# Linear attention feeding a routed expert layer: rests of the kv sums on row halves, one PSUM ring for two projections, and a new hand-made list of steps

## The chip, the core and the metric

The kernel runs on one core of one Trainium2 chip. The metric is the time of one execution in microseconds (us), the median of several runs. The engines named below are TensorE (PE in the profile, its weight loads PEld), VectorE (DVE), ScalarE (ACT), GpSimd (POOL) and the queue that issues most transfers (SP).

## What is computed

Attention without a softmax over positions, for 8 batches x 8 heads of 576 positions, and then a layer of 8 experts in which each of the 4608 tokens goes to one expert:

```python
def phi(x):
    proj = np.einsum('bhsd,df->bhsf', x, w_phi)
    proj = proj - np.max(np.abs(proj), axis=-1, keepdims=True)
    return np.concatenate([np.exp(proj), np.exp(-proj)], axis=-1)
q_p, k_p = phi(q), phi(k)
kv  = np.einsum('bhsf,bhsd->bhfd', k_p, v)
z   = np.sum(k_p, axis=2)
num = np.einsum('bhsf,bhfd->bhsd', q_p, kv)
den = np.einsum('bhsf,bhf->bhs', q_p, z)[..., None] + 1e-06
x = (num / den)                        # then tokens x 512
logits = x @ w_gate + modality_bias[modality_id]
e_idx = argmax(logits); gate = softmax(logits)[e_idx]
out[mask] = gate * (relu(x[mask] @ w1[e]) @ w2[e])     # for each expert e
```

## The kernel before

The 64 heads are worked in 16 groups of four heads (two pairs); a group's number is the `qi` behind the dot in the list of steps below. For each group there are these steps, and each step is one part of a Python generator, so that steps of different groups can be recorded between one another:

- `K0`, `K1`, `K2`: the projection of k. `K0` and `K1` take four tiles of 128 positions, `K2` the last 64 positions of each pair. Parts: matmuls into PSUM (`pk`, L557), the largest absolute value (`mk`, DVE L561), its subtraction (`dk`, DVE L566), two exponentials into `kp` (ACT L572).
- `Q0`, `Q1`: the projection of q for a pair. Matmuls into `pq` (L584) and a copy to SBUF (`d`, ACT L588), twice; the largest over partitions (`mq`, GpSimd L592); a subtraction (DVE L595); two exponentials into `qp` (ACT L601).
- `V`: the sums kv and z. For each sign `s` of the exponential and each head `a`: two matmuls of the rest, the last 64 positions of both pairs (L613; `vb` holds the rests of v of both pairs side by side with zeros, so 130 columns move through weights of 128 rows x 64 columns), then 16 matmuls over the eight full tiles (L617, 65 columns each). One PSUM tile for each `s`, each copied by ACT (L623).
- `T`: kv is transposed (`kvT`, L633), copied, and multiplied with the gate's weights (L642), and DVE puts the result back beside kv.
- `N0` to `N3` and `L`: numerator, denominator and gate sums for 128 positions (`pn`, L668) or for the rests (`pl`, L687). DVE divides and SP stores x (`xs` L676, `xl` L697).
- `XR`, `XL`, `R`: logits and the places of the tokens in the experts' lists, eight times with four or five tiles of tokens (`Route.group`).

The rest of the list (`SU`, `F`, `E`, `W`, `M`, `S`, `Y`, `U`, ...) is the routing plan and the first two slots of the expert layer. After it the expert layer runs slot by slot in a fixed order (`Experts.slots`), which the change leaves alone.

The order is a list written out as text (`ORDER`), 1153 words such as `K2.0`; `program` goes through it and records one part of the named step, and each engine then does its instructions in that order, waiting only for what it needs. Loads of k, q and v aren't in this list: `step` records the load of a group two places on as soon as the last matmul that reads the buffer has been recorded (`READS`). PSUM has eight banks: a ring of four one-bank tiles, `pm`, for `V`, `T`, `N`, `L` and small things; one two-bank tile `pk`; one two-bank tile `pq`.

Ahead of the list stand the loads of groups 0 and 1, and the constructors of `Numbers`, `Route` and `Attention`: 12 and then 16 matmuls on a tile of ones (L88, L102), small DVE operations that make indices, and fills of `pad` and `xg` by GpSimd.

An fp32 matmul shows in the trace as two records. A shape such as `128*64` is the weights' rows and columns; weights of 64 rows (`64*128`) use a half of the array's rows, those of 64 columns a half of its columns, and two halves can be at work at a time.

## Time and profile before

| | us |
|---|---|
| median of 3 runs (lowest 712.62, highest 714.45) | 714.27 |
| the profiled execution | 713.8 |
| its span, from the first to the last instruction | 712.0 |
| PE busy in the span | 696.6 |
| DVE busy | 562.9 |
| ACT busy | 453.0 |
| GpSimd busy | 278.9 |

The first 260 us are the attention steps, then the expert layer takes over. The records of matmuls are pipelined: one lasts some 220 ns while the next begins 30 ns later, so a busy PE in this table can still be waiting, and it is read from starts of blocks and from the waits. A row of the timeline is: start, length of the whole merged piece, engine, line, operation, output and input, number of records, and in brackets the idle time ahead of it.

### The profile page before, as it was taken

To read this page: it belongs to the slowest core of one execution; us is meant where nothing else is said; L and a number is where in the kernel's file an instruction comes from. 1 tells how busy PE (TensorE), PEld (TensorE's weight loads), DVE (VectorE), ACT (ScalarE), POOL (GpSimd) and SP (SyncE) were. 2 spreads that over 40 slices of the span, in tenths; PEclk is the share of its full clock that TensorE was granted. 3 is DMA by queue.
4 is the path that set the end of the run, shared out by engine and by line. 5 is a ranking of instruction groups with operands and counts; after the bars stand their busy time and mean duration, and the time that the engine had idled before them with its cause. 6 is when DMAs were issued, how large, how long until landed. Compare 5 with 4: busy or idle time off the path is not lost.

```text
span 712.0 us, 21360 instructions
## 1 busy us (share of the span) xinstructions
PE 696.6 (98%) x8678; PEld 602.6 (85%) x8678; DVE 562.9 (79%) x1287; ACT 453.0 (64%) x744; POOL 278.9 (39%) x161
## 2 busy tenths in 40 slices
PE   7999999999999999999999999999999999999995
PEld 5889888898888899988888888878888888888884
DVE  7888879899999988579987787768568568678774
ACT  4888688777985883445755576547447447455742
POOL 4555446465445722488742410321131131222122
PEclk9999999999999999999999999999999999999998
DMA  9655555565554668566676739995998984476411
GB/s 217 174 160 159 158 149 152 141 165 159 159 159 111 203 239 276 176 245 205 195 253 237 258 137 417 414 415 181 385 337 330 392 294 139 168 286 227 169 45 32
DMA packets 70321, 155.16 MB, mean 218 GB/s; under 512 B 16698, under 2 KB 45502, under 8 KB 58432
## 3 DMA queue, kind: packets, MB, share of 16 engines
q1 hardware_dynamic: 62208, 134.61, 56.2%
q0 software_dynamic: 7552, 18.92, 7.4%
q8 instruction: 72, 1.18, 0.7%
q14 instruction: 41, 0.34, 0.1%
q10 hardware_dynamic: 448, 0.11, 0.1%
HBM read 135.96 MB, written 19.55 MB: 218 GB/s over the span
## 4 chain that ended last, share of the span: by engine, by line
PE 80%; issue 8%; DVE 6%; ACT 2%; POOL 1%; DMA 1%; SPq 0%; POOLq 0%; ACTq 0%; DVEq 0%
PE p L895 19%; PE p L875 13%; PE pn L668 9%; PE pv L617 7%; PE p L877 6%; PE pq L584 5%; PE pk L557 5%; PE p L858 3%; DVE l L823 3%; PE pv L613 2%; PE pt L831 2%; PE pt L895 2%; PE pt L1005 1%; PE up L991 1%; PE kvT L633 1%
## 5 line engine op out<-in xcount | busy, mean ns | idle before, releaser
L823 DVE TENSOR_TENSOR l<-raw,h 128x1024 fp32r<-128x1024 f32 x148 | 177.1, 1218 | 13.0 <-ACT h L821 12.8
L592 POOL PARTITION_ALL_REDUCE mq<-d x32 | 130.8, 4089 | 115.2 <-ACT d L588 89.9
L821 ACT CAST h<-raw 128x1024 fp32r<-128x1024 f32 x148 | 149.2, 1049 | 3.0 <-PE pt L895 2.2
L875 PE MATMUL p<-xx,h 128*128 128x512 f32 x512 | 140.1, 395 | 0.2 <-issue 0.2
L878 ACT COPY ts<-p 128x256 f32<-128x256 f32 x128 | 47.7, 373 | 110.5 <-PE p L877 109.9
L779 POOL DMA_INDIRECT xg<-x,me x40 | 48.4, 1210 | 163.8 <-PE pt L831 81.4
L895 PE MATMUL p<-h,hh 128*128 128x512 f32 x272 | 107.4, 395 | 0.0
L895 PE MATMUL p<-l,hh 128*128 128x512 f32 x272 | 106.1, 390 | 0.7 <-DVE l L823 0.7
L895 PE MATMUL p<-h,hl 128*128 128x512 f32 x272 | 106.0, 390 | 0.0
L879 DVE TENSOR_TENSOR ts<-ts,p 128x256 f32<-128x256 f32 x128 | 53.5, 418 | 59.5 <-ACT ts L878 59.5
L875 PEld LDWEIGHTS p<-xx,h 128*128 128x128 f32 x512 | 88.0, 189 | 14.3 <-issue 2.0
L877 PEld LDWEIGHTS p<-xx,l 128*128 128x128 f32 x512 | 78.6, 189 | 11.4 <-DVE l L823 0.5
L783 POOL DMA_INDIRECT out_dram<-os,me x36 | 45.7, 1270 | 99.6 <-DVE os L942 72.7
L877 PE MATMUL p<-xx,l 128*128 128x256 f32 x512 | 81.7, 281 | 0.3 <-DVE l L823 0.3
L572 ACT ACTIVATE kp<-dk 128x1024 f32<-128x1024 f32 (+1 forms) x96 | 74.7, 837 | 6.4 <-DVE dk L566 6.3
L668 PE MATMUL pn<-kv,qp 128*64 128x73 f32 x2048 | 73.9, 227 | 0.4 <-DVE kv L645 0.4
L668 PEld LDWEIGHTS pn<-kv,qp 128*64 128x64 f32 x2048 | 68.4, 136 | 5.6 <-issue 2.8
L601 ACT ACTIVATE qp<-d 128x1152 f32<-128x1152 f32 x64 | 71.0, 1159 | 1.4 <-DVE d L595 1.1
L617 PE MATMUL pv<-va,kp 128*64 128x65 f32 x2048 | 70.7, 221 | 0.7 <-issue 0.7
L617 PEld LDWEIGHTS pv<-va,kp 128*64 128x64 f32 x2048 | 68.7, 137 | 0.8 <-issue 0.8
L881 ACT ACTIVATE hh<-ts 128x256 fp32r<-128x256 f32 x128 | 54.1, 423 | 14.3 <-DVE ts L879 14.2
L588 ACT COPY d<-pq 128x576 f32<-128x576 f32 x64 | 40.7, 636 | 32.6 <-PE pq L584 31.6
(234 smaller groups left out, 1109.0 us busy)
## 6 DMA issues: line engine op xcount, KB each, us to landing
raw<-in_w_dram SPq DMA_DIRECT2D x92, 1024.0 KB, 7.0
qt<-in_qT_dram SPq DMA_DIRECT2D x30, 288.0 KB, 4.5
va<-in_vm_dram SPq DMA_DIRECT2D x16, 512.0 KB, 5.1
x<-xs SPq DMA_DIRECT2D x64, 128.0 KB, 3.7
kt<-in_kT_dram SPq DMA_DIRECT2D x15, 512.0 KB, 4.6
kt<-in_kT_dram SPq DMA_DIRECT2D x16, 64.0 KB, 4.7
vb<-in_vt_dram SPq DMA_DIRECT2D x32, 32.0 KB, 4.3
x<-xl SPq DMA_DIRECT2D x32, 32.0 KB, 2.8
```

What stands on the lines that cost most here:

```text
L572: nc.scalar.activation(kp[:, 4 * u:4 * u + T, :, s, :].rearrange("p t a f -> p a t f"), dk, AF.Exp, scale=sc)
L592: self.line.put(nc.gpsimd.partition_all_reduce(mq.rearrange("p a s -> p (a s)"), d.rearrange("p a s -> p (a s)"), P, bass_isa.ReduceOp.abs ...
L601: nc.scalar.activation(qp[:, 2 * pr:2 * pr + 2, i, :], d, AF.Exp, scale=sc)
L617: nc.tensor.matmul(pt[c:c + CW, k // 4, a], kp[:, k, a, s, c:c + CW], va[:, k // 4, k % 4, h], start=False, stop=k == 7, tile_position=(0, c))
L668: nc.tensor.matmul(pp[c:c + CW, g], q["qp"][:, g, s, P * j + c:P * j + c + CW], q["kv"][:, s, g // 2, 73 * (g % 2):73 * (g % 2) + 73], sta ...
L821: nc.scalar.copy(h, r)
L823: nc.vector.tensor_tensor(l, r, h, ALU.subtract)
L875: nc.tensor.matmul(pp, h1[:, cc, f], self.XX[:, cc].rearrange("p a t -> p (a t)"), start=cc == 0, stop=False)
L877: nc.tensor.matmul(pp[:, 0:256], l1[:, cc, f], self.XH[:, cc], start=False, stop=cc == 3)
L879: nc.vector.tensor_tensor(s, s, pp[:, 0:256], ALU.add)
L881: a = nc.scalar.activation(self.HH[:, j], s, AF.Relu)
L895: nc.tensor.matmul(pp, a[:, f, tk], b[:, f], start=i == 0, stop=i == 23)
```

## The change

- **Rests on row halves.** `va` now has nine tiles; the ninth holds the rest of pair 0 in rows 0 to 63 and that of pair 1 in rows 64 to 127. There is one PSUM tile for each pair `r` (not for each sign), both taken at the beginning of `V`. All eight matmuls of the rests come first, as a part of their own, 64 rows each, with weights of 128 columns and 65 columns moving, the two row halves in turn. `V` has five parts instead of four. `vb` and its zeros are gone, and its two loads are one.
- **One ring.** The projections of k take their tile from `pq`, which gets two buffers; `pk` is gone. Only in group 0 do `K1` and `K2` take `pm` tiles, as before.
- **Loads as steps.** `LK`, `LQ`, `LV`, `LA`, `LB` (halves of the first k), `LP` (projection weights, now half on SP and half on ACT's queue), `LG`, `LM` stand in the list. `READS` is gone.
- **Small work as steps.** `NU`, `NA`, `NR` are the parts of the constructors' small operations. `PI.4` is four matmuls on 64 rows of ones into a `pm` tile; it stands in the list 12 times, eight of them ahead of the first `N`. The 16 matmuls of L102 are gone.
- **Routing by nine tiles.** `R` runs four times with nine tiles instead of eight times with four or five; `low` is made by one DVE operation for nine tiles instead of one for each.
- **The list** is another one, with 1200 words.

```diff
+    def idle(self, n, rows=P):
+        pw = self.ps.tile([P, 512], F32, tag="pm", name="idle")
+        for _ in range(n):
+            self.nc.tensor.matmul(pw[:, 0:256], self.one[:rows], self.one[:rows].unsqueeze(1).to_broadcast([rows, 2, P]), start=True, stop=True)
...
-        for _ in range(WARM2):
-            nc.tensor.matmul(pw[:, 0:256], self.one, self.one.unsqueeze(1).to_broadcast([P, 2, P]), start=True, stop=True)
...
-        for t in range(T0, T0 + T):
-            nc.vector.tensor_scalar(self.low[:, t], self.row, self.lof[:, t:t + 1], None, ALU.is_equal)
+        nc.vector.tensor_tensor(self.low[:, T0:T0 + T], self.row.unsqueeze(1).to_broadcast([P, T, P]),
+                                self.lof[:, T0:T0 + T].unsqueeze(2).to_broadcast([P, T, P]), ALU.is_equal)
...
-        self.va = [lv.tile([P, 2, 4, 130], F32, name=f"va{i}") for i in range(2)]
-        self.vb = [lv.tile([P, 2, 130], F32, name=f"vb{i}") for i in range(2)]
+        self.va = [lv.tile([P, 9, 130], F32, name=f"va{i}") for i in range(2)]
...
+    def load_w(self):
+        for a, e in enumerate((self.nc.sync, self.nc.scalar)):
+            e.dma_start(self.wp[64 * a:64 * a + 64], self.w_phi)
...
-    def load_a(self, qi, vm):
-        self.nc.sync.dma_start(self.va[qi % 2][:, :, :, 1:129], vm[qi])
-
-    def load_b(self, qi, vt):
-        for j in range(2):
-            r = slice(64 * j, 64 * j + 64)
-            self.nc.sync.dma_start(self.vb[qi % 2][r, j, 1:129], vt[qi, r])
+    def load_v(self, qi, vm, vt):
+        va = self.va[qi % 2]
+        self.nc.sync.dma_start(va[:, 8, 1:129], vt[qi])
+        self.nc.sync.dma_start(va[:, 0:8, 1:129], vm[qi].rearrange("p r t d -> p (r t) d"))
...
-            pv = [pk.tile([P, 2, 4, P], F32, tag="pk", name=f"pk{n}_{u}")[:, :, 0:T]]
+            pv = [pq.tile([P, 2, 512], F32, tag="pq", name=f"pk{n}_{u}").rearrange("p a (t f) -> p a t f", f=P)[:, :, 0:T]]
...
-        va, vb, kp = self.va[qi % 2], self.vb[qi % 2], q["kp"]
+        va, kp = self.va[qi % 2], q["kp"]
+        pt = [pm.tile([P, 512], F32, tag="pm", name=f"pv{n}_{r}")[:, 0:260].rearrange("p (s a c) -> p s a c", s=2, a=2)
+              for r in range(2)]
         for s in range(2):
-            pt = pm.tile([P, 512], F32, tag="pm", name=f"pv{n}_{s}")[:, 0:260].rearrange("p (r a c) -> p r a c", r=2, a=2)
             for a in range(2):
-                h = slice(65 * a, 65 * a + 65)
-                for c in range(0, P, CW):
-                    nc.tensor.matmul(pt[c:c + CW, :, a], kp[:, 8, a, s, c:c + CW], vb[:, :, h],
-                                     start=True, stop=False, tile_position=(0, c))
-                for k in range(8):
-                    for c in range(0, P, CW):
-                        nc.tensor.matmul(pt[c:c + CW, k // 4, a], kp[:, k, a, s, c:c + CW], va[:, k // 4, k % 4, h],
-                                         start=False, stop=k == 7, tile_position=(0, c))
-            yield
-            if s == 0:
+                for r in range(2):
+                    i = slice(64 * r, 64 * r + 64)
+                    nc.tensor.matmul(pt[r][:, s, a], kp[i, 8, a, s], va[i, 8, 65 * a:65 * a + 65],
+                                     start=s + a == 0, stop=False)
+        yield
+        for r in range(2):
+            for s in range(2):
+                for a in range(2):
+                    for k in range(4):
+                        for c in range(0, P, CW):
+                            nc.tensor.matmul(pt[r][c:c + CW, s, a], kp[:, 4 * r + k, a, s, c:c + CW],
+                                             va[:, 4 * r + k, 65 * a:65 * a + 65],
+                                             start=False, stop=s + a + k == 5, tile_position=(0, c))
+            yield
+            if r == 0:
                 q["kv"] = w.tile([P, 2, 2, 146], F32, tag="kv", name="kv" + n)
-            nc.scalar.copy(q["kv"][:, s, :, 8:138], pt.rearrange("p r a c -> p r (a c)"))
+            nc.scalar.copy(q["kv"][:, :, r, 8:138], pt[r].rearrange("p s a c -> p s (a c)"))
             yield
...
-    K2.0 K2.0 SU.0 SU.0 K0.0 K0.0 Q0.0 Q0.0 K2.0 K1.0 Q0.0 K2.0 Q0.0 Q0.0 K0.0 K0.0 K0.1 K1.0 K0.1 Q1.0 Q1.0 Q1.0 Q1.0
+    NU.0 NU.0 LA.0 LP.0 NU.0 LQ.0 NU.0 NU.0 K0.0 NU.0 LB.0 PI.4 NA.0 NA.0 NA.0 K0.0 Q0.0 K1.0 K0.0 K2.0 Q0.0 Q1.0 NU.0
...
-        pk = pool(pr, "pk", "right", space=PSUM)
-        pq = pool(pr, "pq", "right", space=PSUM)
+        pq = pool(pr, "pq", "right", bufs=2, space=PSUM)
...
+                if u == "PI":
+                    num.idle(qi, 64)
+                    continue
```

What the new list makes of the order is seen at three places. The first is PE at the start of the program. Before, from the last of the L102 matmuls to the first full tiles of `V` of group 0 (the first number behind `pk`, `pq` and `pv` is the group):

```order
L557 MATMUL pk0_2_0_257<-wp_126,kt0_234 128x128
L557 MATMUL pk0_2_1_258<-wp_126,kt0_234 128x128
L557 MATMUL pk0_0_270<-wp_126,kt0_234 128x128 x8
L584 MATMUL pq0_0_0_281<-qt0_238,wp_126 128x288 x2
...
L584 MATMUL pq0_1_1_334<-qt0_238,wp_126 128x288 x2
L584 MATMUL pq1_0_0_341<-qt1_249,wp_126 128x288 x2
L557 MATMUL pk1_1_351<-wp_126,kt1_243 128x128 x8
L613 MATMUL pv0_0_371<-vb0_207,kp0_305 64x2x65 x2
L617 MATMUL pv0_0_371<-va0_205,kp0_305 64x65 x16
```

And now, from the same engine's first projection to the same tiles:

```order
L585 MATMUL pk0_0_174<-wp_76,kt0_164 128x128 x8
...
L612 MATMUL pq0_0_0_197<-qt0_169,wp_76 128x288 x2
...
L612 MATMUL pq0_1_1_249<-qt0_169,wp_76 128x288 x2
L585 MATMUL pk1_0_262<-wp_76,kt1_246 128x128 x8
...
L585 MATMUL pk1_1_292<-wp_76,kt1_246 128x128 x8
L113 MATMUL numbers_301<-mean_273,free_70 128x8
L650 MATMUL pv0_0_280<-va0_128,kp0_255 64x65 x32
L650 MATMUL pv0_1_281<-va0_128,kp0_255 64x65 x32
```

The same projections stand ahead of `V` of group 0; the first is `K0` instead of `K2`, and the 16 matmuls on ones ahead of it are gone, while four-matmul idle pieces (left out here) stand between.

The second is PE in the middle of the attention part, around `V` of group 10. Before:

```order
L613 MATMUL pv10_0_3370<-vb0_207,kp10_3005 64x2x65 x2
L617 MATMUL pv10_0_3370<-va0_205,kp10_3005 64x65 x16
L613 MATMUL pv10_0_3370<-vb0_207,kp10_3005 64x2x65 x2
L617 MATMUL pv10_0_3370<-va0_205,kp10_3005 64x65 x16
L687 MATMUL pl9_3407<-kv9_3008,qp9_3110 64x73 x8
L557 MATMUL pk11_2_3424<-wp_126,kt11_2832 128x128 x2
L584 MATMUL pq11_0_0_3439<-qt11_2986,wp_126 128x288 x2
L613 MATMUL pv10_1_3446<-vb0_207,kp10_3005 64x2x65 x2
```

Now:

```order
L642 MATMUL pv10_1_3153<-va0_128,kp10_3027 128x65
L612 MATMUL pq11_0_0_3162<-qt11_2726,wp_76 128x288 x2
L702 MATMUL pn9_2_3165<-kv9_2939,qp9_2845 64x73 x16
L721 MATMUL pl9_3182<-kv9_2939,qp9_2845 64x73 x8
L650 MATMUL pv10_0_3152<-va0_128,kp10_3027 64x65 x32
L612 MATMUL pq11_0_1_3237<-qt11_2726,wp_76 128x288 x2
L585 MATMUL pk11_0_3251<-wp_76,kt11_2563 128x128 x8
L702 MATMUL pn9_0_3260<-kv9_2939,qp9_2845 64x73 x16
L650 MATMUL pv10_1_3153<-va0_128,kp10_3027 64x65 x32
```

The rests stand as a block of their own between projections, and both PSUM tiles of `V` are held from there to the end of the second block of L650.

The third is the queue SP around the load of v for group 12 (`va0` in both; `xl9` and `xl10` are stores of group 9 and 10). Before:

```order
L534 DMA va0_205<-in_vm_dram 128x8x128
L539 DMA vb0_207<-in_vt_dram 64x128 x2
L697 DMA x_58<-xl9_3434 64x128 x2
L520 DMA qt13_3626<-in_qT_dram 64x2x576 x2
L697 DMA x_58<-xl8_3364 64x128 x2
...
L676 DMA x_58<-xs10_1_3762 128x256
L697 DMA x_58<-xl10_3790 64x128 x2
```

Now:

```order
L710 DMA x_58<-xs10_1_3718 128x256
L710 DMA x_58<-xs10_0_3686 128x256
L731 DMA x_58<-xl10_3730 64x128 x2
L566 DMA va0_128<-in_vt_dram 128x128
L567 DMA va0_128<-in_vm_dram 128x8x128
L559 DMA kt14_3838<-in_kT_dram 128x2x512
```

The load of v for group 12 stood ahead of group 10's stores of x and now stands behind all of them.

## Rows read from the trace of the kernel before

**Rows 1.** The page: span, and the engines' busy time, share and instructions
```profile
span 712.0 us, 21360 instructions
PE 696.6 (98%) x8678; PEld 602.6 (85%) x8678; DVE 562.9 (79%) x1287; ACT 453.0 (64%) x744; POOL 278.9 (39%) x161
```

**Rows 2.** Busy time by stretches: engine, (instructions), then PE's clock, transfers' share, GB/s
```profile
20.00:40.00 20.00, 19.95 (x459) 17.24 (x456) 16.80 (x37) 17.22 (x25) 8.78 (x4) 1.00 0.54 137
...
220.00:240.00 20.00, 19.81 (x451) 17.04 (x449) 19.70 (x63) 14.86 (x21) 14.68 (x6) 1.00 0.45 127
```

**Rows 3.** Waits of PE, 28 to 300 us: total us, times, longest
```profile
PE pv L617 <- issue: 0.7, 1, 0.7
PE pk L557 <- PE pq L584: 0.5, 2, 0.3
PE pn L668 <- DVE kv L645: 0.4, 1, 0.4
```

**Rows 4.** Waits of PE from 300 us to the end
```profile
PE p L895 <- DVE l L823: 0.7, 1, 0.7
PE p L877 <- DVE l L823: 0.3, 1, 0.3
PE p L875 <- issue: 0.2, 1, 0.2
```

**Rows 5.** Timeline of the start, all engines
```profile
0.75 0.88 SPq L529 DMA_DIRECT2D kt<-in_kT_dram  x2
...
1.34 0.61 ACTq L484 DMA_DIRECT2D wp<-in_w_phi_dram  x1
...
4.62 3.58 PE L102 MATMUL warm<-one 128*128 128x256 bf16 x16
...
8.12 1.54 PE L557 MATMUL pk<-wp,kt 64*128 64x128 f32 x20
...
10.22 0.64 ACT L588 COPY d<-pq 128x576 f32<-128x576 f32 x1 [6.74 <-PE pq L584]
```

**Rows 6.** Transfers of the whole run: times, KB each, median us from issue to landing
```profile
va<-in_vm_dram SPq DMA_DIRECT2D x16, 512.0 KB, 5.1
...
kt<-in_kT_dram SPq DMA_DIRECT2D x2, 256.0 KB, 3.0
...
wp<-in_w_phi_dram ACTq DMA_DIRECT2D x2, 32.0 KB, 3.2
```

**Rows 7.** Chain of work that ended last: start, us, piece
```profile
262.72 11.71 PE p L858 x96
```

**Rows 8.** Timeline of PE, the first `pn`
```profile
27.89 3.25 PE L668 MATMUL pn<-kv,qp 128*64 128x73 f32 x96
```

**Rows 9.** Timeline of PE, 100 to 109 us
```profile
101.15 1.16 PE L557 MATMUL pk<-wp,kt 64*128 64x128 f32 x16
102.14 0.66 PE L584 MATMUL pq<-qt,wp 64*128 64x288 f32 x4
...
103.28 0.59 PE L642 MATMUL kvT<-wgb,kvTs 128*64 128x16 f32 x16
103.72 1.22 PE L668 MATMUL pn<-kv,qp 128*64 128x73 f32 x32
...
105.45 1.06 PE L557 MATMUL pk<-wp,kt 64*128 64x128 f32 x16
106.36 0.76 PE L584 MATMUL pq<-qt,wp 64*128 64x288 f32 x4
...
107.32 1.10 PE L617 MATMUL pv<-va,kp 128*64 128x65 f32 x32
108.25 0.40 PE L613 MATMUL pv<-vb,kp 128*64 128x130 f32 x4
108.48 1.10 PE L617 MATMUL pv<-va,kp 128*64 128x65 f32 x32
```

**Rows 10.** Weight loads by form, 0 to 300 us: count, busy us, mean ns, idle before
```profile
L617 PEld LDWEIGHTS pv<-va,kp 128*64 128x64 f32 x2048 | 68.7, 137 | 0.8 <-issue 0.8
...
L557 PEld LDWEIGHTS pk<-wp,kt 64*128 64x128 f32 x576 | 38.3, 188 | 8.5 <-issue 2.5 <-PE pq L584 1.4 <-DVE dk L566 1.3
```

**Rows 11.** DVE by form, 0 to 300 us, the longest operation
```profile
L595 DVE TENSOR_TENSOR d<-d,mq 128x1152 f32<-128x1152 f32 x32 | 46.0, 1438 | 2.2 <-POOL mq L592 2.1
```

More of the change, by code (lines that the diff above doesn't have):

```diff
@@ L85, in __init__, with ops @@
         nc.gpsimd.partition_all_reduce(m, z, P, bass_isa.ReduceOp.absmax)
-        pw = ps.tile([P, 512], F32, tag="pm", name="warm")
-        for _ in range(WARM):
-            nc.tensor.matmul(pw[:, 0:256], self.one, self.one.unsqueeze(1).to_broadcast([P, 2, P]), start=True, stop=True)
-        self.free = w.tile([P, P], F32, name="free", bufs=1)
+        self.idle(WARM)
+    def ops(self):
+        nc, w = self.nc, self.w
         nc.vector.memset(self.free[:, 0:1], 0.0)
+        yield
         n = 1
@@ L94, in __init__ @@
             n *= 2
+            yield
         mean = w.tile([P, 8], F32, name="mean", bufs=1)
         nc.vector.memset(mean, 1.0 / P)
-        pp = ps.tile([P, 512], F32, tag="pm", name="numbers")[:, 0:8]
+        yield
+        pp = self.ps.tile([P, 512], F32, tag="pm", name="numbers")[:, 0:8]
         nc.tensor.matmul(pp, self.free, mean, start=True, stop=True)
-        pw = ps.tile([P, 512], F32, tag="pm", name="warm2")
-        for _ in range(WARM2):
-            nc.tensor.matmul(pw[:, 0:256], self.one, self.one.unsqueeze(1).to_broadcast([P, 2, P]), start=True, stop=True)
@@ L140, in __init__ @@
-        self.one = num.one
-        self.oh = [c.tile([P, T + 1, E], BF16, name=f"oh{T}") for T in (4, 5)]
-        for t in self.oh:
-            nc.vector.memset(t, 0.0)
-        idf = w.tile([P, NT // 9, 9], F32, name="idf", bufs=1)
-        g = w.tile([P, NT // 9], F32, name="first", bufs=1)
-        t = w.tile([P, 4], F32, name="tile", bufs=1)
-        nc.vector.tensor_scalar(g, num.free[:, 0:NT // 9], 2.0 * S, num.part, ALU.mult, ALU.add)
-        nc.vector.tensor_scalar(t, num.free[:, 0:4], float(P), None, ALU.mult)
@@ L165, in __init__, with load, ops @@
         self.me = c.tile([P, 2 * EARLY, 2], I32, name="me")
+    def load(self, j):
+        if j == 0:
+            self.nc.sync.dma_start(self.m2, self.mod.bitcast(I32).rearrange("p (t w) -> p t w", w=2))
+        else:
+            self.nc.sync.dma_start(self.bb, self.bias_in.rearrange("m e -> (m e)").partition_broadcast(P)
+                                   .rearrange("p (m e) -> p m e", m=2))
+    def ops(self):
+        v, w, num, idf = self.nc.vector, self.w, self.num, self.idf3
+        v.tensor_copy(self.k, num.free[:, 0:MOST])
+        yield
+        v.tensor_scalar(self.w8, self.e, -1.0, float(E), ALU.mult, ALU.add)
+        yield
+        v.tensor_scalar(self.ecap, self.e, float(CAP), None, ALU.mult)
+        yield
+        v.tensor_copy(self.base, self.ecap)
+        yield
+        v.tensor_scalar(self.k256, self.k, 256.0, None, ALU.mult)
+        yield
+        v.tensor_scalar(self.k32, self.k[:, :UM], float(UR), None, ALU.mult)
+        yield
+        v.tensor_copy(self.row, num.free)
+        yield
+        v.memset(self.oh, 0.0)
+        yield
+        g = w.tile([P, NT // 9], F32, name="firsts", bufs=1)
+        t = w.tile([P, 4], F32, name="tile", bufs=1)
+        v.tensor_scalar(g, num.free[:, 0:NT // 9], 2.0 * S, num.part, ALU.mult, ALU.add)
+        yield
+        v.tensor_scalar(t, num.free[:, 0:4], float(P), None, ALU.mult)
+        yield
+        sh = [P, NT // 9, 4]
+        v.tensor_tensor(idf[:, :, 0:4], g.unsqueeze(2).to_broadcast(sh), t.unsqueeze(1).to_broadcast(sh), ALU.add)
+        yield
+        v.tensor_scalar(idf[:, :, 4:8], idf[:, :, 0:4], float(S), None, ALU.add)
+        yield
+        for j in range(2):
+            r = slice(64 * j, 64 * j + 64)
+            v.tensor_scalar(idf[r, :, 8], g[r], float(512 + j * (S - 64)), None, ALU.add)
+            yield
+        v.tensor_copy(self.meta.bitcast(I32)[:, :, 1], idf.rearrange("p g t -> p (g t)"))
+        yield
     def clear(self, xg):
```

285 lines of the change are left out of this document (133 added, 152 removed).

## The prediction

> **What bounds the kernel now.** I read the page's engine table first: PE is busy 98% of the span, DVE 79%, ACT 64%, GpSimd 39% [rows 1]. A busy PE proves little, since records of matmuls overlap, so the second view is the waits. From 28 us to 300 us PE's largest waits are 0.7, 0.5 and 0.4 us, 1.6 us together [rows 3]; from there to the end they are 0.7, 0.3 and 0.2 us, 1.2 together [rows 4]. The stretches say the same: PE fills 19.95 of 20 us early and 19.81 late in the attention part, at a granted clock of 1.00, while DVE has 16.80 and 19.70 and ACT 17.22 and 14.86 [rows 2]. So from 28 us on PE goes from block to block, and what is saved on DVE, ACT or GpSimd is worth nothing while PE doesn't wait for it. Three things can move the end: PE's own work, waits that the new order brings to it, and the time at which its first real work begins.
>
> The start is the one stretch with a hole. The data of the first projection is there early: the weights are issued at 1.34 us [rows 5] and land a median of 3.2 us later [rows 6], at 4.54; the first k is issued at 0.75 and takes 3.0, to 3.75. But PE starts its 16 matmuls on ones at 4.62, needs 3.58 us for them, and comes to the first projection at 8.12 [rows 5]. These are 0.224 us each, against 11.71/96 = 0.122 us for each of the expert layer's matmuls of 256 columns [rows 7], about twice: the start ran at the lower of the two clocks, 1.2 and not 2.4 GHz.
>
> **The start after the change.** The 16 matmuls on ones go; eight idle pieces of four stand between projections ahead of the first `N`, on 64 rows, in places where PE would wait for ACT or for loads. The first projection can then start at 4.5 us, 3.6 us earlier. Not all of it comes through. PE's work at the start runs at the low clock until the clock rises, whatever the work is, and eight idle pieces are 32 matmuls, 32 x 0.122 = 3.9 us at the high clock, twice what stood there in number; where the list puts one in a gap it is free, elsewhere it costs 0.49 us. And from 10 us on ACT has to copy and exponentiate: it first copies at 10.22, after 6.74 us of waiting for PE [rows 5], and then is 86% busy from 20 to 40 us [rows 2]. ACT starts some 2 to 3 us earlier (a copy of q follows `K0` and not `K2` and `K0`), and this, not PE, paces the stretch until the first `pn`, at 27.89 us [rows 8]. I take 2.0 us as what is left of the lead: **-2.0**, with -3.6 (all of it) and -0.5 (nearly all eaten by idle pieces) as ends.
>
> **The rests.** Before, 4 records of L613 take 0.23 us from start to start (108.25 to 108.48 [rows 9]), four times in a group: 0.92 us, 57 ns a record. After, they are 8 matmuls, 16 records, with half as many columns moving (65 for 130) but weights of 128 columns on 64 rows. No row shows that pair, so the question is what sets the pace. Two rows answer it in part: 16 records of L642 with 16 columns moving take 103.28 to 103.72, 27.5 ns each, and 32 records of L617 with 65 columns take 107.32 to 108.25, 29 ns each [rows 9]. Four times the columns cost nothing, so with weights of 64 columns the load sets the pace. A load of 128 columns is longer (188 ns against 137 in the trace's own measure [rows 10]), and the projection of k, weights of 64 rows x 128 columns as the new rests have, goes at 0.91/16 = 57 ns (105.45 to 106.36 [rows 9]). By that row the new rests cost 0.91 us a group, and the gain is 0.01 x 16 = **-0.2 us**. Had the moving columns set that 57 ns (there it is 128 of them), 65 columns would take 0.46 us, and the gain would be 16 x 0.46 = -7.2 us. Those are the ends; I take the first, as it is the row of the same weights, and the pace of L642 speaks for weights.
>
> The Trainium skill bears on this (TensorE: Matmul & The Clock Gate, section on LDWEIGHTS, loading the stationary operand): the time of a weight load follows its columns, not its rows, so that a load of few rows and 128 columns costs as much as a full one. By this rule the change halves what moves and not what is loaded, and the term stays at -0.2; the rows of L642 and L617 agree, and no row here has 64 rows, 128 columns and only 65 moving.
>
> **Changes of the weights' shape.** A block of 16 records of k takes 0.99 us when blocks of full rows stand ahead (101.15 to 102.14), and 0.91 between blocks of its own shape (105.45 to 106.36 [rows 9]): 0.08 us for a change of shape. Counted in the order that the two kernels give PE up to the first expert matmul, there are 111 places before where the weights go from column halves to row halves or back, and 97 after. 14 x 0.08 = **-1.1 us**.
>
> **Late idle pieces.** Four stand behind the first `N`, in the stream that PE doesn't leave: 4 x 4 x 0.122 = 2.0 us if none falls into a wait, 0 if all do. There were waits of 1.6 us to fall into [rows 3]; **+1.0**.
>
> **The ring.** Two two-bank tiles serve both k and q where each had one. Before, k waited for q's block 0.5 us in all [rows 3]; with two buffers a projection finds one free if the copy of the last but one is through. **-0.5**, and 0 or a little more than nothing at the other end, since a slow `mk` on DVE now holds a buffer that q wants.
>
> **What `V` holds.** Both PSUM tiles of `V` are taken at the rests and given back after the second block and its copy, and in the order around `V` of group 10 a projection of q, `pn`, `pl` and a second `pq`, `pk` and `pn` stand between. With PE's paces of [rows 9] (some 0.9 us for rests, 0.9 for k, 0.93 twice for each pair's tiles, 0.9 for a `pn` of 32 records) that is about 7 us of two of four `pm` tiles. Before, one tile was held, for 0.23 + 0.93 twice, 2.3 us, two times a group. What is left for `pn`, `pl` and `kvT` in those 7 us is two tiles, each emptied by DVE, whose longest operation, the subtraction of L595, lasts 1.44 us [rows 11]. I take nothing for this, for in that stretch PE has other blocks between two of `pn`; its price stands with the rivals.
>
> **DVE and the queues.** Routing by nine tiles and one operation for `low` take some operations from DVE, whose 19.70 of 20 us [rows 2] hardly ever held PE up: 0.4 us in all [rows 3]. Nothing. On SP, loads of v stand behind the stores of x of the group that ends, as for group 12; a load waits in line for stores whose DVE work isn't done. Its landing takes 5.1 us [rows 6]. For k of groups 7 and 10 and v of 12 and 15 the new list puts the load only 20 to 33 words ahead of its use, by my estimate from the blocks of [rows 9] little more than 4 us of PE's work, where it was at least 60 words before. At the start the store of the padding waits for a fill by GpSimd that now stands behind GpSimd's first maximum, and on SP the gate's weights and the loads of v and q of group 1 stand behind that store. What is queued there is needed only at the second group, well past 20 us. I take nothing, and 1 us for each late load as the bad end.
>
> The part from 300 us on, and the tail behind PE's last matmul, aren't touched.
>
> **Sum.** -2.0 - 0.2 - 1.1 + 1.0 - 0.5 = -2.8 us on the profiled 713.8, so 711.0; the median of the runs stood 0.5 us above that execution (714.27), so **711.5 us**. With each term at its better or worse end the forecast's own spread is 709 to 713.5.
>
> **Rivals.** *A, the rests at half the pace's price:* weights for one row half are loaded while the other half works, and the moving columns set the pace, 0.46 us a group. Then -7.2 in the place of -0.2: 704.5 us. For it: a block of k with 128 columns moving and 128 loaded can't tell which of them took its 57 ns. Against it: L642's pace doesn't follow its moving columns. The Trainium skill has this as a rule (TensorE: Matmul & The Clock Gate, Part 3, row/col tiling): weight loads overlap with matmuls in flight when their row groups differ; the trace of before can't say whether that carries here.
>
> *B, the lead is given back:* of the start 1 us is left, and two or three loads or idle pieces hold PE up 1 us each: -1.0 - 0.2 - 1.1 + 1.0 + 1 = -0.3 on 714.27, **714** us. For it: short leads of loads behind stores; a PE so full that it has no slack to win the time back. Against: the buffers of k, q and v are two deep, and most loads still stand far ahead of their use.
>
> *C, slower:* the two held tiles make `pn` or `kvT` wait for DVE in each group. The price is up to a third of the 1.44 us subtraction that stands in DVE's line, 0.5 us x 16 groups = 8 us: 711.5 + 8 = **719.5**. It decides, past what a measurement hides, from (716.4 - 711.5)/16 = 0.31 us a group. For it: DVE is filled 19.70 of 20 us late in the part [rows 2], so a divide or copy on it is often queued. Against: PE waited for DVE 0.4 us in 272 us before [rows 3], and the new list has 97 changes of shape and not more, that is, larger runs of like work.
>
> **How the numbers follow.** About 0.3%, 2.1 us, is what a measurement can tell from no change: 712.1 to 716.4 counts as the same. The forecast has 0.45, with four fifths of it below 712.1; A 0.13; B 0.25, nearly all within; C 0.17, nearly all above. Faster 0.36 + 0.12 = 0.48, same 0.09 + 0.24 + 0.01 = 0.34, slower 0.18. The range reaches from A's upper half, 705, to C's lower half, 718: it leaves out about a half of A and of C, some 15 in 100 together. The forecast's own, 709 to 713.5, stands beside it.
>
> **What would show it.** The first projection of k starts at 4.5 to 5 us, ACT's first copy near 8, and the first `pn` at 25 to 27 us; 16 records of the rests take about 0.9 us from their start to the next block's (0.46 if A holds); PE's waits from 28 to 300 us stay under 2 us; the expert part is as long as before. It is wrong if `pn`, `pl` or `kvT` wait for DVE 0.3 us or more in each group (C), if a transfer of k or v is the releaser of PE's waits (B), or if the idle pieces stand behind work that was ready.

## The result: slower, and the profile after

The changed kernel takes 724.14 us (median of 4 runs, 721.58 to 726.23) where the kernel before takes 713.65: a ratio of 1.0144 with a 95% interval of 1.0115 to 1.0173. That is 1.4% slower. The prediction of 711.5 us, and its range of 705 to 718, were wrong. The profiled execution took 723.39 us, 721.3 of it the span. The page of the changed kernel, engines' busy time, against [rows 1]:

```profile
span 721.3 us, 21289 instructions
PE 696.2 (97%) x8702; PEld 605.7 (84%) x8702; DVE 559.3 (78%) x1195; ACT 452.8 (63%) x740; POOL 280.4 (39%) x161
```

PE does as much as before, and the span is 9.3 us longer. Where the time went is told by PE's waits from 28 to 300 us (total us, times, longest), to be held against [rows 3]:

```profile
PE pt L863 <- DMA xg<-x,me: 5.0, 2, 3.4
PE pn L702 <- DVE me L371: 1.7, 1, 1.7
PE pq L612 <- issue: 1.6, 1, 1.6
PE kvT L667 <- ACT kv L657: 1.3, 1, 1.3
PE pn L702 <- DVE gl L693: 1.1, 1, 1.1
PE pv L650 <- issue: 0.9, 1, 0.9
PE pk L585 <- DMA kt<-in_kT_dram: 0.7, 2, 0.4
PE rows L363 <- DVE kv L679: 0.7, 1, 0.7
```

The rows of `kvT`, `pv` and `pk` lie ahead of 205 us. The other five lie between 215 and 274 us, 10.1 us together, in the place where attention ends and the first expert's slot begins; I call it the joint. There the last groups' attention runs beside the routing plan: DVE works out which rows each expert gets (`ids`, `me`), GpSimd issues the gather of these rows (`xg`), and PE transposes them (`pt`). The same place by stretches (PE, its loads, DVE, ACT, POOL; then PE's clock), against [rows 2]:

```profile
220.00:240.00 20.00, 18.94 (x455) 16.89 (x453) 19.67 (x60) 13.68 (x21) 7.90 (x2) 1.00 0.08 26
240.00:260.00 20.00, 16.69 (x471) 15.70 (x469) 18.15 (x52) 14.25 (x19) 13.27 (x4) 1.00 0.55 181
260.00:280.00 20.00, 15.88 (x261) 15.45 (x262) 12.83 (x38) 8.60 (x10) 6.84 (x7) 0.91 0.90 311
```

DVE is full to 250 us while PE has holes, and then both have them. The plan's rows and the first gather, in the kernel before and in the changed one:

```profile
232.15 0.18 DVE L344 TENSOR_REDUCE me<-rows 128x12 f32<-128x36 f32 x1
233.89 1.16 POOL L779 DMA_INDIRECT xg<-x,me  x1 [0.18 <-issue]
```

```profile
249.53 0.18 DVE L371 TENSOR_REDUCE me<-rows 128x12 f32<-128x36 f32 x1
251.27 1.17 POOL L811 DMA_INDIRECT xg<-x,me  x1 [0.17 <-DVE rd L689]
```

From 300 us on PE waits 0.8, 0.3 and 0.2 us, as in [rows 4].

**A measure for the rest of this text.** The two lists have different orders, so equal instructions can't be compared. I weigh each PE record by the mean start-to-start time of its kind in the trace of before (50 ns for a record of `pk`, 28 for one of `pv`), leave out rests and ones, and see when two kernels have done the same work. The table says how late each kernel is when it has done what one trace of the kernel before (before_again) had done at its 205, 245 and 278 us (worked out from the traces, in us; a kernel loses time where its number grows):

```
                205    245    278
before          1.6    1.6    1.7
after           0.6    2.6   10.0
after_again     4.5    6.5   11.6
after_3         1.4    3.0    9.2
after_4         5.5    7.5   15.7
plan_early      3.2   16.6   17.9
both_moves      5.4   15.9   18.3
turns_late      2.2    3.9    9.2
turns_2         3.9    5.6   10.7
short_fill      2.5    1.2    5.1
no_last_max     1.4    0.3    5.1
long_fill       2.1    0.1    6.3
dk_next         1.7    1.1    6.5
dk_turns        2.8    1.7    5.5
dk_turns_2      4.9    3.8   10.2
fill_turns      2.4    1.0    3.7
no_ones         1.0    2.2    5.0
rests_alone    12.5   13.3   15.4
before_no_max   1.4    1.3    1.1
```

The changed kernel's four traces lose 7.1 to 10.2 us from 205 to 278, the kernel before 0.1. Ahead of 205 they scatter by 5 us, and most of that is the start.

How far to trust the table: with other weights (medians, or with and without the steps between blocks) the columns of 205 and 278 move by 1 us or so. The column of 245 lies beside a wait of 1.7 us (`pn` for `me`, above), and there the changed kernel's first trace stands anywhere from 2.5 to 5.1. So the two halves of the joint can't be told apart well, and I read from 205 to 278. Each row is one execution: those of after_4 and dk_turns_2 took 6.8 us more than the medians of their runs.

### The profile page after: what moved, and what is told of

Same layout as the page of the kernel before. It is cut to its first block, busy times and chain, and to the rows that moved or that the text cites. A ratio compares the mean times of both kernels' runs of the same rounds, so it can differ in the third digit from the quotient of the medians.

```text
span 721.3 us, 21289 instructions
## 1 busy us (share of the span) xinstructions
PE 696.2 (97%) x8702; PEld 605.7 (84%) x8702; DVE 559.3 (78%) x1195; ACT 452.8 (63%) x740; POOL 280.4 (39%) x161
## 3 DMA queue, kind: packets, MB, share of 16 engines
q8 instruction: 72, 1.18, 0.7%
## 4 chain that ended last, share of the span: by engine, by line
PE 60%; DVE 10%; issue 8%; DMA 3%; ACT 1%; POOL 1%; SPq 0%; POOLq 0%; DVEq 0%; ACTq 0%
PE p L927 19%; PE p L907 12%; PE p L909 6%; PE pn L702 4%; PE p L890 3%; PE pv L650 3%; DVE l L855 2%; PE pk L585 2%; PE pq L612 2%; DMA xg<-x,me 2%; PE pt L863 2%; PE pt L927 2%; PE pt L1037 1%; PE up L1023 1%; DMA kt<-in_kT_dram 1%
## 5 line engine op out<-in xcount | busy, mean ns | idle before, releaser
L702 PE MATMUL pn<-kv,qp 128*64 128x73 f32 x2048 | 75.8, 230 | 2.7 <-DVE me L371 1.7
L702 PEld LDWEIGHTS pn<-kv,qp 128*64 128x64 f32 x2048 | 69.9, 138 | 8.7 <-issue 7.3
L650 PE MATMUL pv<-va,kp 128*64 128x65 f32 x2048 | 65.6, 222 | 0.9 <-issue 0.9
L650 PEld LDWEIGHTS pv<-va,kp 128*64 128x64 f32 x2048 | 62.4, 138 | 2.8 <-issue 2.0
L927 PEld LDWEIGHTS p<-l,hh 128*128 128x128 f32 x272 | 51.1, 188 | 11.4 <-DVE l L855 1.3
```

Of the source, the lines that this page charges most:

```text
L650: nc.tensor.matmul(pt[r][c:c + CW, s, a], kp[:, 4 * r + k, a, s, c:c + CW], va[:, 4 * r + k, 65 * a:65 * a + 65], start=False, stop=s + a ...
L702: nc.tensor.matmul(pp[c:c + CW, g], q["qp"][:, g, s, P * j + c:P * j + c + CW], q["kv"][:, s, g // 2, 73 * (g % 2):73 * (g % 2) + 73], sta ...
L927: nc.tensor.matmul(pp, a[:, f, tk], b[:, f], start=i == 0, stop=i == 23)
```

## The experiments

Theory 1: the loss is made at the joint, where DVE and GpSimd make the plan and the gather late, either by the plan's place in the list (1a) or by DVE standing still beside GpSimd's search for the largest over partitions, the maximum (1b). Rivals: PSUM held in each group (case C), the rests, the loads. Ratios are to the kernel before on the same chip. That takes 714 us on some chips and 722 to 724 on others, so times from different chips aren't compared; no_ones, rests_alone, turns_late and no_last_max ran on one of the second kind, dk_next, turns_2, dk_turns and fill_turns on another, after_4 and dk_turns_2 on a third. Lags from different kinds of chip are to be held against each other with care: no_ones, the old list on one of the second kind, loses 4.0 us from 205 to 278, where the kernel before loses 0.1 on a faster one.

**The two kernels again.** No edit.

> The kernel before, unchanged, so that its trace stands beside the next three from the same chip. If the chips differ, its PE waits here are longer than the 1.6 us of its first trace, and at the same places of the program; if they don't, it has the same waits.

> The changed kernel, unchanged, on the same chip as the one above. Theory 1 (the loss lies at the joint between attention and the first slot, from 205 to 280 us): level with or up to 2.5 us ahead of the kernel before in work done until 205 us, then some 10 us lost. Rival (PE waits a little everywhere, because two PSUM tiles are held in each group): the lag grows group by group from 40 us on.

Measured 0.9994 (0.9984 to 1.0005) and 1.0145 (1.0088 to 1.0201). The changed kernel's lag hardly grows group by group: 3.0 us at 60 us and 4.5 at 205, under 0.2 a group where case C needs 0.31, then 7.1 more. Case C is out for the new list.

**The two parts that can be had alone.** no_ones is the kernel before with `WARM2 = 0`; rests_alone is

```diff
+        pt = [pm.tile([P, 512], F32, tag="pm", name=f"pv{n}_{r}")... for r in range(2)]
...
-            pt = pm.tile([P, 512], F32, tag="pm", name=f"pv{n}_{s}")...
...
-                    nc.tensor.matmul(pt[c:c + CW, :, a], kp[:, 8, a, s, c:c + CW], vb[:, :, h], ...
...
+                    nc.tensor.matmul(pt[r][:, s, a], kp[i, 8, a, s], vb[i, r, 65 * a:65 * a + 65], ...
```

> The kernel before without the 16 matmuls on ones ahead of the first projection, nothing else. Theory (the start gives some 2 us): first projection at 4.6 us, 1 to 2.5 us less in all, about 711.8. Rival (vector and scalar engine set the pace of the start): first projection at 4.6 us but the first numerator within 0.5 us of 27.9, no change.

> The kernel before with the rests of the kv sums on row halves, one PSUM tile for each pair, all eight matmuls ahead of the full tiles; list and rings as before. Theory (the weight load sets the pace, and two changes of shape in each group are added at 0.08 us): 16 records take 0.84 us as in the changed kernel for 0.92, so -1.3 + 2.6 = +1.3 us at worst and -1.3 at best: no change that can be measured. Rival A (half the pace): 0.46 us for the 16 records, 7 us less.

no_ones: 1.0051 (1.0032 to 1.0070), no gain but a little slower; at 205 us it is 1.0 late, between the two traces of before (0 and 1.6). Its first projection starts at 5.79 us, and not at 4.6, and takes 2.51 us where the kernel before needs 1.54 for the same 20 records behind its ones [rows 5]:

```profile
5.79 2.51 PE L557 MATMUL pk<-wp,kt 64*128 64x128 f32 x20 [1.02 <-DMA kt<-in_kT_dram]
```

That is the lower of PE's two clocks (1.2 GHz; the granted clock is full from 11.9 us): 111 ns from record to record, 69 in the kernel before. The first numerator comes at 28.19 us, as the rival had it, so the earlier start was lost again. The ones don't settle the clock either: with them, before_no_max has 111 ns too.

rests_alone: 1.0172 (1.0141 to 1.0203), much slower, which neither expectation had. Here the lag does grow, from 2.0 us at 33 us to 12.5 at 205, some 0.95 us in each of 11 groups, while no_ones with the same list stays at 1.0. Three of its PE waits from 28 to 300 us (no_ones has none at `pv`):

```profile
PE pv L614 <- issue: 2.6, 3, 1.2
PE pn L672 <- issue: 1.9, 4, 0.7
PE pv L614 <- DVE gs L663: 1.3, 2, 1.0
```

Twice, 1.3 us together, `pv` waits for a PSUM tile that DVE still reads (`gs`), which is case C's mechanism in a list that wasn't made for two held tiles. It names only a small part of the 10.5 us: other waits are "issue", no releaser in the trace, and the added changes of shape should make some 0.16 us a group (2 x 0.08, my estimate from [rows 9]). The rest of that loss stays open. The new list, with the rests as a block of their own, doesn't have it.

**Moving the transposes.** turns_late and turns_2 (the same kernel) move two words:

```diff
-T.15 TU.0 T.15 ... L.15 N2.14 XS0.0 ... N0.15 TV.0 N0.15 M0.0 ... M2.0 XV0.0
+T.15 T.15 ... L.15 N2.14 TU.0 XS0.0 ... N0.15 N0.15 M0.0 ... M2.0 TV.0 XV0.0
```

> The changed kernel with two words of its list moved: the first transposes of the gathered tokens (TU) stand behind the numerators of group 14 instead of ahead of them, and the second (TV) behind the first slot's first products. Theory 1 (the loss lies at the joint: PE stands at the transposes until a gather lands, 3.4 and 1.7 us, and then runs some 10 us at a lower clock): both waits go and the clock stays, 5 to 7 us less than the changed kernel, about 718. Rival (PE had the work to do anyway and the wait moves to the copies behind the transposes): at most 1.5 us less, about 723.

> The changed kernel with TU and TV moved, as in turns_late, now on the chip of the others. Theory 1: 2 to 4 us less than the changed kernel (the lag gained from 250 to 280 us falls from about 5 us to 2 or 3), the four waits from 215 to 252 us stay. Rival: no gain.

1.0072 (1.0046 to 1.0098) and 1.0058 (1.0037 to 1.0079), beside 1.0044 (1.0020 to 1.0067) for the changed kernel on a third chip of that kind (after_4): by ratios no gain that shows. Both waits at the transposes are gone, and from 205 to 278 us 7.0 and 6.8 us are lost instead of 7.1 to 10.2. The four waits ahead of them stay, as expected. The waits for the gather were at most a third of the loss; they vary, too, with 5.0, 0.8, 2.0 and 3.5 us in the changed kernel's four traces.

PE's clock changed with it: over 255 to 280 us the granted clock is 0.93 in the changed kernel's first three traces and 1.00 in the fourth; in the first it falls to the lower level at 264.2 us, behind the wait of 3.4 us at the transposes. In turns_late and turns_2 it is 1.00, as in the kernel before.

**The plan earlier.** plan_early draws the words of R.11, F, E, SU and XG together; both_moves adds the two words above.

> The changed kernel with the words of the early plan (R.11, F, E, SU between them and XG) drawn together towards the first R.11, so that the first gather's word stands some 70 words earlier; nothing else. Theory 1a (the plan's place in the vector engine's order makes the gather late): rows of the plan done and the gather issued 8 us or more earlier than 249.7 and 251.3 us, no wait at the first transposes, 3 to 6 us less than the changed kernel beside it. Rival (beside GpSimd's maximum the plan's operations stand still wherever the list puts them): gather less than 3 us earlier, at most 1.5 us less.

> The plan drawn together as above, and both groups of transposes behind other work (TU behind the numerators of group 14, TV behind the first slot's first products). Theory 1: both waits go, the clock stays, 6 to 9 us less than the changed kernel, and with the lead of the start about as fast as the kernel before on this chip or 2 us faster. Rival: as plan_early alone.

1.0264 (1.0242 to 1.0287) and 1.0183 (1.0157 to 1.0210): much slower, so an earlier plan is no cure, and theory 1a falls. In plan_early the first gather was issued at 244.05 us, 7 earlier than in the changed kernel, and PE paid for it. Waits of PE in plan_early (some left out are "issue"):

```profile
PE pq L612 <- issue: 2.6, 1, 2.6
PE rk L287 <- DVE oh L272: 2.1, 1, 2.1
PE rows L363 <- DVE gs L693: 2.0, 1, 2.0
...
PE idle L88 <- DVE gs L693: 1.3, 1, 1.3
PE pn L702 <- DVE gl L693: 1.3, 1, 1.3
```

The four that name DVE make 6.7 us, where the changed kernel has 3.5. The first of them stands behind an operation of 2.47 us at 214.87, of a kind that comes up next. There was no room on DVE: what the plan takes earlier, the attention gets later. So the question is what fills DVE.

**What fills DVE.** DVE's timeline of the changed kernel has four operations that last 2 us and more in the joint, each behind a start of GpSimd's maximum (first DVE, then POOL):

```profile
212.09 2.47 DVE L266 SCALAR_TENSOR_TENSOR sc<-l,w 128x72 f32<-128x72 f32 x1
...
221.81 2.16 DVE L386 TENSOR_TENSOR cste<-cete,nse 128x8 f32<-128x8 f32 x1
...
231.82 3.60 DVE L623 TENSOR_TENSOR d<-d,mq 128x1152 f32<-128x1152 f32 x1
...
247.11 2.51 DVE L370 TENSOR_SCALAR me<-ids 128x12 int32<-128x12 f32 x1
```

```profile
212.00 3.97 POOL L620 PARTITION_ALL_REDUCE mq<-d  x1 [2.56 <-ACT d L616]
221.51 3.94 POOL L620 PARTITION_ALL_REDUCE mq<-d  x1 [5.54 <-ACT d L616]
231.75 3.96 POOL L620 PARTITION_ALL_REDUCE mq<-d  x1 [6.29 <-ACT d L616]
240.16 10.94 POOL L620 PARTITION_ALL_REDUCE mq<-d  x2 [4.45 <-ACT d L616]
```

Elsewhere the first takes 0.23 us, the second 0.16, the third 1.34 (dk_next, below) and the fourth 0.17 (short_fill), and the second has eight columns. Each ends 2.5 to 2.6 us after a maximum began, the subtraction 3.7; less their own lengths, all four were let go 2.3 to 2.4 us into it. The row of 240.16 is two maxima, the second from 247.08, and 3.94 us each elsewhere: the first was held up by 3.1 us, while four DVE operations with two inputs in SBUF ran, the first of them begun 0.03 us ahead of it:

```profile
240.13 1.35 DVE L623 TENSOR_TENSOR d<-d,mq 128x1152 f32<-128x1152 f32 x1
241.40 1.97 DVE L357 TENSOR_TENSOR what<-inslot,part 128x540 bf16<-128x540 bf16 x3
```

In the kernel before no DVE operation of 1.5 us stands from 205 to 262 us. Beside one of its maxima there, operations that read PSUM aren't touched:

```profile
216.12 1.22 DVE L561 TENSOR_REDUCE mk<-pk 128x8 f32<-128x1024 f32 x1
...
216.47 3.94 POOL L592 PARTITION_ALL_REDUCE mq<-d  x1 [7.83 <-ACT d L588]
...
217.37 1.22 DVE L566 TENSOR_TENSOR dk<-pk,mk 128x1024 f32<-128x1024 f32 x1
```

The Trainium skill has this (SBUF — State Buffer, Who interferes with whom): a vector operation in a mode that takes two ports contends with GpSimd, one with two inputs in SBUF contends with a GpSimd operation that reads SBUF, and whoever starts first keeps the other waiting. The trace agrees on both directions, with 2 us of standing for DVE and 3 us for GpSimd. It differs in the length, for the page has the lock held for the whole instruction, and here DVE is let go about 2.3 us into a maximum of 3.94. Nor is that all of it: in the kernel before, a cast that began 2.45 us into a maximum (151.37 us) stood until that ended:

```profile
153.82 1.51 DVE L282 CAST lof<-lor 128x4 f32<-128x4 int32 x1
```

To test it, no_last_max and short_fill (one kernel) leave the maximum out for groups 12 to 15, long_fill keeps GpSimd busy as long with hardly any reading (a copy of two columns of `d`, then four fills), and before_no_max leaves the same maxima out of the kernel before:

```diff
+        if qi >= 12:
+            self.line.put(nc.gpsimd.memset(mq, 3.0))
+        else:
             self.line.put(nc.gpsimd.partition_all_reduce(...
```

> The changed kernel, but for groups 12 to 15 the largest over partitions is left out: GpSimd fills the tile with a constant. Theory 1b (the plan is late because vector operations with two SBUF inputs stand still for about 2.2 us beside the first part of GpSimd's maximum, four times between 212 and 250 us, and the gather stands behind the last two maxima on GpSimd): no vector operation over 2 us from 205 to 260 us, the rows of the plan done 7 us or more earlier than 249.7 us, the gather issued before 245 us, no wait at the transposes, 5 to 8 us less in all. Rival (the list simply puts the plan late): rows of the plan less than 3 us earlier, at most 2 us less in all.

> The changed kernel, unchanged, beside the next three on the same chip. All theories: about 1.0145 of the kernel before; vector operations of 2 us and more beside GpSimd's maximum at the same four places between 205 and 260 us (shares w, first count, the subtraction of the maximum, the rows' copy).

> The changed kernel, but for groups 12 to 15 the largest over partitions is left out and GpSimd fills the tile with a constant (the same kernel as in the run without the last maxima). Theory 1b (the standing vector operations cost the joint): 7 to 10 us less than the changed kernel on the same chip, that is within 0.4% of the kernel before. Rival (that earlier run stood well only because its chip was slower for the kernel before): less than 4 us below the changed kernel.

> As short_fill, but GpSimd first copies two columns of the projection, so that it starts when the maximum would start, and then fills the tile four times, so that it is busy for about 4 us as with the maximum but hardly reads the buffer. Theory 1b-read (what hurts is that GpSimd reads while vector operations read two tiles): as fast as short_fill within 1.5 us, no vector operation over 2 us. Rival 1b-queue (what hurts is that GpSimd is occupied, so that the subtraction and the gather come late): as slow as the changed kernel within 2 us. Rival 1b-any (any GpSimd work stops such vector operations): vector operations of 2 us and more remain.

> The kernel before with the largest over partitions left out for groups 12 to 15 in the same way. If the stalls cost only where the new list puts two-tile vector operations beside the start of a maximum: within 2 us of the kernel before. Rival (the maxima cost either list the same): 7 us or more below it.

no_last_max: 1.0007 (0.9987 to 1.0027). On one chip after_3 1.0151 (1.0118 to 1.0184), short_fill 1.0042 (1.0028 to 1.0056), long_fill 1.0089 (1.0060 to 1.0117), before_no_max 0.9994 (0.9984 to 1.0004). So 8.1 of 11.1 us hang on the maxima of four groups in the new list (725.11 to 717.02, before 714.05), and nothing that shows in the old one. (The two profiled executions differ by 3.9 us alone, and from 205 to 278 they lose 7.8 and 2.6.) In long_fill GpSimd's work was 4.4 us long, and no vector operation over 2 us stands in the joint; up to 245 us it keeps pace with short_fill, so it is the reading that hurts there, 5 us of the 8 by the medians. Behind that it loses what short_fill doesn't, 3 us, since its fills keep the gather back:

```profile
244.70 4.42 POOL L623 MEMSET mq<- 128x1152 f32 x4
249.29 2.30 POOL L817 DMA_INDIRECT xg<-x,me  x1 [0.18 <-issue]
```

```profile
258.34 0.30 PE L869 MATMUL pt<-ident,xg 128*128 128x128 f32 x1 [3.74 <-DMA xg<-x,me]
```

In short_fill the plan's rows are done 4.0 us earlier than in the changed kernel (7 were expected of the same kernel, no_last_max), the gather is issued at 245.92 us, 5.4 earlier than 251.27, and PE waits 0.2 us for it. So two of the three in the expectation hold, each for a part: GpSimd's reading holds up DVE (1b-read), and GpSimd's being busy holds up the gather (1b-queue).

**The cure with nothing left out.** dk_next moves five words, so that operations which read PSUM stand at the starts of four maxima; dk_turns adds the two words of turns_late; fill_turns is short_fill with those two:

```diff
-SU.0 K0.14 R.11 ... R.11 R.11 K0.14 R.11 ... R.11 T.12 K0.14 T.12
+SU.0 K0.14 K0.14 K0.14 R.11 ... R.11 R.11 R.11 ... R.11 T.12 T.12
-E.0 L.12 K1.14 L.12 ... N3.12 K1.14 N0.12
+E.0 L.12 K1.14 K1.14 L.12 ... N3.12 N0.12
-T.13 K0.15 T.13 Q0.14 ... Q0.14 K0.15 T.13
+T.13 K0.15 K0.15 T.13 Q0.14 ... Q0.14 T.13
-E.0 K1.15 E.0 K1.15 Q1.15
+E.0 K1.15 K1.15 E.0 Q1.15
```

> The changed kernel with five words of its list moved, all of them vector work: the largest and the subtraction of K0.14 ahead of a step of R.11, and the subtractions of K1.14, K0.15 and K1.15 right behind their maxima, so that at four starts of GpSimd's maximum the vector engine reads from PSUM instead of two tiles in SBUF. Theory 1b: of the four vector operations over 2 us between 205 and 260 us at least three are gone, the waits of PE of 1.6, 1.1, 0.7 and 1.7 us between 215 and 252 us shrink to under 2 us together, 3 to 5 us less than the changed kernel (1.0145), about 1.009 of the kernel before. Rival (such an operation is met at every place, whatever the order): other operations stand still in their place, less than 1.5 us gained.

> The five vector words of dk_next and the two of turns_late together, nothing left out. Theory 1 (two causes that add): 6 to 8 us less than the changed kernel, 1.002 to 1.006 of the kernel before. Rival (one hides the other): as the better of the two alone.

> short_fill (the largest over partitions left out for groups 12 to 15) with TU and TV moved as in turns_late. Theory 1: 2 to 4 us less than short_fill's 1.0042, level with the kernel before within 0.3% (712 to 716 where that takes 714). Rival (a third cause in the joint): 717 us and more.

1.0038 (1.0017 to 1.0058), 1.0001 (0.9986 to 1.0016) and 0.9991 (0.9974 to 1.0007). Three of the four operations that stood still are short now, and the fourth stands 1.18 us instead of 2.51 (DVE in dk_next, maxima at 213.29, 221.15 and 230.88 us and a pair from 239.17):

```profile
213.45 1.23 DVE L589 TENSOR_REDUCE mk<-pk 128x8 f32<-128x1024 f32 x1
...
214.78 1.23 DVE L594 TENSOR_TENSOR dk<-pk,mk 128x1024 f32<-128x1024 f32 x1
...
215.92 0.23 DVE L266 SCALAR_TENSOR_TENSOR sc<-l,w 128x72 f32<-128x72 f32 x1
...
224.47 0.16 DVE L386 TENSOR_TENSOR cste<-cete,nse 128x8 f32<-128x8 f32 x1
...
233.26 1.34 DVE L623 TENSOR_TENSOR d<-d,mq 128x1152 f32<-128x1152 f32 x1
...
246.51 1.18 DVE L370 TENSOR_SCALAR me<-ids 128x12 int32<-128x12 f32 x1
```

Of the waits of 1.6, 1.1, 0.7 and 1.7 us one is left, 1.2 us, and from 205 to 278 us dk_next loses 4.8 where the changed kernel loses 7.1 to 10.2.

Four of these kernels ran on one chip, so their times stand side by side (medians): turns_2 727.28, dk_next 724.87, dk_turns 722.26, fill_turns 721.05, the kernel before 722.28. The five vector words, which change nothing but DVE's order, take 5.0 us off (turns_2 to dk_turns); leaving the maxima out instead takes 6.2 off (turns_2 to fill_turns). The five also free the projections' PSUM tile earlier, and what that alone is worth wasn't tried. The two words of the transposes take 2.6 off (dk_next to dk_turns), and with them the granted clock from 255 to 280 us is 1.00 and not 0.93.

The changed kernel itself hadn't run on that chip, so it and the seven words ran on another together:

> The changed kernel, unchanged, beside dk_turns_2. If the chip is one on which the kernel before takes 714 us: 1.0145 of it, about 724.5. If it is one on which that takes 722 to 724: 1.005 to 1.010, since there the kernel before loses some 8 us behind 290 us that the changed kernel's order does not lose.

> The seven moved words, nothing left out. Two causes that add: 4.5 to 7 us less than the changed kernel beside it (718 to 720 where that takes 724.5). Rival (the level time on the other chip came from the slower kernel before alone): less than 2 us.

after_4 1.0044 (1.0020 to 1.0067), dk_turns_2 0.9986 (0.9966 to 1.0006): 726.92 and 723.38 us, 3.5 less, short of the 4.5 that I had set but past the rival's 2. On this chip the kernel before is itself 10 us slower than on others, so these ratios flatter the new list. From 205 to 278 us dk_turns and dk_turns_2, the same kernel, lose 2.7 and 5.3 us (in the second the clock is at the lower level from 251 to 254 us) instead of the changed kernel's 7.1 to 10.2. On a chip where the kernel before takes 714 us the seven words weren't run; 5 of 11 us less would leave them some 6 us slower than it there, by my estimate from these lags. No version here beats the kernel before.

## Why the prediction was wrong, step by step

- **DVE and the queues, taken at nothing.** This is the step that failed. I argued that DVE's 19.70 of 20 us had hardly held PE up (0.4 us). That is what an engine without slack looks like one step ahead of the limit: it says that the old order fitted, not that another would. At the joint the plan, DVE's, was on the path to the gather, and I didn't follow that chain: rows of the plan ready at 232.3 us and gather at 233.89 before, 249.7 and 251.27 after. Nor did I ask what DVE does beside GpSimd's maxima, though the list decides that. Measured: +9.4 us from 205 to 278 (0.6 to 10.0, the kernel before 1.6 to 1.7). Of these some 5 hang on the maxima, that is, on vector operations that stand beside them and on what they delay (2.6 lost in short_fill for 7.8 in after_3; 5.0 for the five words on one chip); the transposes' place, in three of four traces with the lower clock behind it, is 2 to 3 (2.6 on one chip); of the rest I know only waits of PE that the profile calls "issue", inside blocks.
- **The start, -2.0.** The first projection came at 4.05 us and not at 8.12, and ACT's first copy at 8.12, as forecast; but the first `pn`, forecast for 25 to 27 us, came at 28.30. At 33 us the changed kernel is 1.1 ahead (0.3 by other weights) and before 0.7 behind the common trace, 1.0 to 1.8 us. But in after_again it is 2.0 late. Four idle matmuls tell why (first the changed kernel's profile, then after_again's):

```profile
5.37 0.60 PE L88 MATMUL idle<-one 64*128 64x256 bf16 x4
```

```profile
5.90 1.06 PE L88 MATMUL idle<-one 64*128 64x256 bf16 x4
...
12.42 1.51 PE L88 MATMUL idle<-one 64*128 64x256 bf16 x7
```

  In one execution PE has the pace of the higher clock by 5.4 us (109 ns from one idle matmul to the next), in the other that of the lower one (213 ns), and its record of the granted clock reaches the full level at 4.8 us in one and 13.6 in the other, with the same program. The kernel before scatters too: 8.5 us there, 4.2 in before_again. So a lead of up to 1.8 us is there in one trace and not in others, and no_ones, which takes only the ones away, has none. That the -2.0 is near the first trace's lead is luck.
- **The rests, -0.2.** Sixteen records of L642 take 202.92 to 203.76, 0.84 us (0.94 at some places), against 0.92: -1.3 at best. Rival A's 0.46 isn't there; half the moving columns left the pace almost as it was (57 to 52.5 ns a record), so the weights set most of it. (A's own sum was off a little: 16 x 0.46 is 7.4.)

```profile
202.92 1.01 PE L642 MATMUL pv<-va,kp 64*128 64x65 f32 x16
203.76 0.71 PE L612 MATMUL pq<-qt,wp 64*128 64x288 f32 x4
```

- **Changes of shape -1.1, idle pieces +1.0, ring -0.5.** Together with the rests they should have given 0.8 us from 33 to 205 us. The changed kernel lost 0.8 net of before's 0.9 in that stretch (1.7 against 0.9), and after_again 2.5; by other weights it is 0.3 and 1.2, so these terms can't be settled one by one. The loads of k for groups 7 and 10 were late, as rival B had it, by 0.4 us each here and group 10's by up to 1.3 elsewhere, and `kvT` waited 1.3 for ACT. The ring's -0.5 became +1.6 (one of the five waits of the joint): at 218 us a `pq` block, "issue" by the profile, began 0.1 us behind DVE's subtraction from the `pk` that held the other buffer, the cost that I had put at "a little more than nothing"; in dk_next, where that subtraction comes earlier, the wait is gone.
- **Case C (719.5)** had the sign and named DVE, but in each group and by PSUM alone; between 28 and 205 us `pn` never waited for DVE. Case B's 1 us for a late load was about right. The range missed because every case left the joint as it was.

## What to carry to other kernels

When a list is reordered, follow the chain that ends a phase (here logits, plan, gather, transposes) through every engine in both orders, and price an engine that is 98% busy at its next delay, not at its past waits. Beside a GpSimd operation that reads SBUF, place vector work that reads PSUM; a two-input operation of eight columns cost 2 us there. Early work for a late engine is no gain when the engine that does it is full.

## What was not expected of the hardware

- The lock between DVE and GpSimd caught operations of 8 to 1152 columns, and GpSimd lost 3.1 us to it once. A maximum holds DVE up in two pieces: what began in its first 2.3 us was let go then, and the cast that began 2.45 us into one stood until that ended.
- Some of PE's "issue" waits stand at the same place of a program in each trace, with lengths that differ: behind the eleventh record of a `pv` block at 31 to 34 us every trace of the new list has one, of 0.3 to 2.2 us. Others come and go. In no_ones one in the expert layer took

```profile
310.41 0.77 PE L895 MATMUL p<-h,hh 128*128 128x512 f32 x1 [5.58 <-issue]
```

  on a chip where the kernel before takes 723.66 us. Whether that is why it is 9 us slower there wasn't tried, since it was profiled only on faster chips.
- After PE stood 3.4 us at the transposes, 32 records of `pn` took 1.68 us (263.86 to 265.54) where 1.07 is usual, and the granted clock of that stretch reads 0.61: here the wait was paid for a second time.
